# Attention and two MLPs on one core: a and b products of three batches moved ahead of the last transposes

## The chip, the cores and the metric

The kernel runs on one core of one Trainium2 chip. The metric is the device time of one execution in microseconds (us), lower is better. Names of the engines: PE is TensorE (PEld its weight loads), DVE is VectorE, ACT is ScalarE, POOL is GpSimd, SP is SyncE, which here only issues DMAs.

## The reference

Three blocks in a row, all in float32 with float64 MLP weights that the kernel splits itself:

```
a    = softmax over the sequence of phi              # 4 batches, 8 heads, 576 positions, 32 memories
k_m  = a^T k,  v_m = a^T v                           # 32 x 64 per head
attn = softmax(q k_m^T / 8) over the 32 memories
x    = attn v_m                                      # as 2304 tokens x 512
x    = ((x @ w_a) * (x @ w_b)) @ w_out               # 512 -> 1536 -> 512
x    = elu(x @ w_in) @ w_out2                        # 512 -> 2048 -> 512
```

## The kernel before

Precision is kept by splitting each float32 operand of a matmul in two float32r parts, hi and lo, and adding three products (hi hi, hi lo, lo hi). The kernel is one hand-written order: inside `tc.manual_schedule()` each engine executes its instructions in the order in which the Python code records them, and semaphores hold an instruction until its inputs are there and its output buffer is free.

**First stage, a loop over the four batches i.** `stage_kv` makes k_m and v_m from a and the loaded k, v (L360), `stage_turn`, `stage_kT` and `stage_vT` turn them, `stage_scores(i-1)` makes the scores of the batch before (L401, L405), `stage_aT(i+1)` transposes a of the next one (L336, evicted by ACT at L340), `stage_softmax` subtracts the maximum (DVE, L427, L429) and takes the exponential (ACT, L431), `stage_norm` divides by the sums (DVE, L445 to L451) and `stage_xT` transposes the result by PE (L462, L466) and splits it into `xhi` (ACT, L69) and `xlo` (DVE, L70). So softmax(b) is recorded in round b+1, norm(b) and xT(b) in round b+2; what is left of batches 2 and 3 stands behind the loop.

**u.** The product attn v_m w_a is done as attn (v_m w_a). `step_u(f, .., bs)` makes u = v_m w for a block f of 128 hidden units and some batches: two halves of 12 matmuls each on PE (L489), each rounded to hi by ACT (L504) and to lo by DVE (L500, one step later by `defer`) into the one buffer `ur`; behind the second `lower` the function `spread` issues four DMAs on SP for each batch (L513), which bring u into the partitions where the next matmul wants it. `step_u(0)` is done in two pieces, batches 0 and 1 in round 3, batches 2 and 3 behind the loop.

**ab.** `steps_ab(f, b)` has two parts of 12 matmuls each (L629): part 0 gives a, which ACT copies to `a_sb` (L636); part 1 gives b, by which DVE multiplies a (L638). One and two steps later ACT and DVE split the product into gh (L639) and gl (L640). 12 blocks f by 4 batches follow each other; `step_u(f+1)` stands behind batch 1 of block f, and `run_o1` (L671) takes up to three finished blocks of a batch into the output y of the first MLP. The second MLP follows (`step_h`, `steps_o2`).

**Weights.** Each weight block (a unit, 512 KB of float64) is loaded by POOL's DMA queue into one of two `raw` buffers (L103) and worked into hi and lo by seven pieces, which `fill(n)` records between other steps. Within unit n: slot 1 takes hi of unit n-1 (ACT, L133), slot 2 its lo (DVE, L142), slot 3 frees the raw buffer and issues the load of unit n+2, slot 4 has ACT convert the low words of unit n+1 (L119), slot 5 its magnitude (L113); the other slots are DVE alone (L155, L158, L163, L168, L173, L176). In the first stage `FILLS` gives the number of pieces for each round, and in the ab steps it is `RATE_AB`, one piece for each part.

**PSUM.** Up to the end of the first stage there are two tiles of two banks (`ps0`, taken by `pstile`) and four of one bank (`ps1`, by `pone`); then `ps1` is closed, and `ps2` gives two more of two banks.

**The end of the first stage** (L581 to L613): u of batches 2 and 3, scores of batch 3, norm and xT of batch 2, softmax and norm of batch 3 in buffers that are borrowed from the pool `pb` (hence the list in `both`, and an identity made again by POOL in `small`); then in the loop over f and b ab(0,0), ab(0,1), u of block 1, xT of batch 3, ab(0,2), ab(0,3), ab(1,0).

Of the kernel before, what the change touches and what calls it, by code (L numbers as in the profile page):

```python
# [21 lines left out]
def attention_then_two_mlps(ctx, tc, q, kv, kv_left, phi, w_ab, w_o1, w_i2, w_o2, out):  # L22
# [179 lines left out]
    FILLS = 6, 6, 6, 6  # L202
# [220 lines left out]
    def stage_softmax(b):  # L423

        for (ps, n, ng), (at, mx, _) in zip(st.pop(("sc", b)), st["at", b]):
            mx = mx[0:n]
            nc.vector.tensor_reduce(out=mx, in_=ps, op=ALU.max, axis=AX.X)  # L427
            for o, i, m in both(at, n, ps, mx):
                nc.vector.tensor_tensor(out=o, in0=i, in1=m.to_broadcast(list(o.shape)), op=ALU.subtract)  # L429
            for o, in both(at, n):  # L430
                nc.scalar.activation(out=o, in_=o, func=AF.Exp, scale=SCALE)  # L431

    def both(at, n, *others):

        if isinstance(at, list):
            yield from ([at[u][0:n], *[x[:, u] for x in others]] for u in range(2))
        else:
            yield [at[0:n], *others]

    def stage_norm(b, eng):  # L440

        parts = [(at, sm[0:n], n) for (at, _, sm), n in zip(st["at", b], (P, LEFT))]
        for at, sm, n in parts:
            for o, m in both(at, n, sm):
                nc.vector.tensor_reduce(out=m, in_=o, op=ALU.add, axis=AX.X)  # L445
        for at, sm, n in parts:
# [25 lines left out]
    def step_u(f, amount, bs=tuple(range(B))):  # L472
# [7 lines left out]
        def half(k):  # L480
# [15 lines left out]
            src = ps.rearrange("p i (c n) -> p i c n", c=2)  # L496
            hi, lo = [ur[:, :, 2 * k:2 * k + 2, x] for x in range(2)]
# [18 lines left out]
        half(0)  # L516
        half(1)

    with tc.manual_schedule():
# [79 lines left out]
        small = pb.tile([P, S], F32R, tag="gl", name="small", bufs=9).bitcast(F32)  # L599
        ats = [pb.tile([P, S], F32R, tag="gh", name=f"at{u}", bufs=9).bitcast(F32) for u in range(2)]  # L600
        ats = [t[:, 0:4 * NJ * M].rearrange("p (g m) -> p g m", m=M) for t in ats]
        als = [small[:, u * P:(u + 1) * P].rearrange("p (g m) -> p g m", m=M) for u in range(2)]
        st["ident"] = small[:, 2 * P:3 * P]
# [292 lines left out]
```

## Time and profile before

| | us |
|---|---|
| three executions, median (lowest, highest) | 838.73 (837.79, 839.49) |
| the profiled execution, its own time | 838.2 |
| its span, first to last instruction | 836.4 |
| PE busy in it | 794.7 |
| DVE busy in it | 610.3 |

The rows read for the prediction stand in a section of their own below. A line of the timeline gives start, duration, engine, line of the kernel, operation, output<-input, shapes and count, and in brackets how long the engine had been idle and what released it. All times count from the start of the span.

### The profile page before, as it was taken

The numbers are of one execution on the slowest core, as the hardware profiler recorded it, in microseconds if no ns is written. First come the engines' busy times: TensorE is split into PE (matmuls) and PEld (weight loads), VectorE is DVE, ScalarE is ACT, GpSimd is POOL, SyncE is SP. The second block draws the span as 40 slices with busy tenths as digits, with TensorE's granted clock in tenths as the row PEclk, the third lists the DMA queues.
The fourth block names the chain that finished last, engine by engine and source line by source line (L and its number), as shares of the span: only waits on it lengthen the run. The fifth ranks groups of instructions, "written<-read, shape, count | busy, mean of one in ns | idle before, by whom it ended". The sixth has DMA issues, their size and how long they took to land.

```text
span 836.4 us, 13805 instructions
## 1 busy us (share of the span) xinstructions
PE 794.7 (95%) x5576; PEld 739.7 (88%) x5576; DVE 610.3 (73%) x1015; ACT 413.6 (49%) x636; POOL 43.1 (5%) x91
## 2 busy tenths in 40 slices
PE   4686799999999999999999999999999999999998
PEld 3575789999999999999999898889998889998896
DVE  4497877878887888567788852887777876776555
ACT  4354456655454444334358753566554565543360
POOL 3000000000000000000000000000000000000000
PEclk9598899999999999999999999999999999999999
DMA  9973267664775277516001200111111110100006
GB/s 302 367 252 91 61 161 178 159 152 109 176 175 125 80 177 177 125 30 150 26 1 51 74 27 1 53 49 52 50 51 51 51 51 25 51 26 1 1 1 226
DMA packets 32175, 82.95 MB, mean 99 GB/s; under 512 B 4848, under 2 KB 4848, under 8 KB 32112
## 3 DMA queue, kind: packets, MB, share of 16 engines
q1 hardware_dynamic: 22320, 46.41, 20.5%
q0 software_dynamic: 9792, 35.66, 14.4%
q8 instruction: 44, 0.72, 0.4%
q14 instruction: 19, 0.16, 0.1%
HBM read 52.17 MB, written 4.72 MB: 68 GB/s over the span
## 4 chain that ended last, share of the span: by engine, by line
PE 87%; DVE 4%; DMA 4%; ACT 2%; issue 1%; SPq 1%; POOL 1%; DVEq 0%; ACTq 0%; POOLq 0%
PE o_ps L796 24%; PE h_ps L753 24%; PE o_ps L671 17%; PE ab_ps L629 16%; DMA raw<-in_w_ab_dram 3%; PE u_ps L489 2%; PE sc L401 2%; PE pk L360 1%; DVE ur L500 1%; SPq L513 1%; DMA u<-ur 1%; DVE a_sb L638 0%; DVE at L429 0%; ACT gh L639 0%; DVE a L163 0%
## 5 line engine op out<-in xcount | busy, mean ns | idle before, releaser
L629 PE MATMUL ab_ps<-xhi,u 128*128 128x288 f32 x768 | 141.0, 301 | 5.3 <-DVE ur L500 2.6
L629 PEld LDWEIGHTS ab_ps<-xhi,u 128*128 128x128 f32 x768 | 116.1, 192 | 7.4 <-DVE ur L500 3.0
L796 PE MATMUL o_ps<-ulh,g2h 128*128 128x512 f32 x288 | 114.2, 397 | 0.0
L796 PE MATMUL o_ps<-ull,g2h 128*128 128x512 f32 x288 | 114.2, 396 | 0.0
L796 PE MATMUL o_ps<-ulh,g2l 128*128 128x512 f32 x288 | 103.5, 397 | 0.0
L771 DVE SCALAR_TENSOR_TENSOR e<-e,th 128x768 f32<-128x768 f32 x48 | 46.0, 959 | 76.5 <-ACT e L768 76.2
L753 PE MATMUL h_ps<-yh,usl 128*128 128x384 f32 x384 | 98.2, 336 | 0.0
L753 PE MATMUL h_ps<-yh,ush 128*128 128x384 f32 x384 | 98.1, 336 | 0.0
L753 PE MATMUL h_ps<-yl,ush 128*128 128x384 f32 x384 | 98.1, 336 | 0.0
L764 ACT ACTIVATE e<-h_ps 128x768 f32<-128x768 f32 x48 | 39.0, 812 | 96.1 <-PE h_ps L753 94.1
L629 PE MATMUL ab_ps<-xlo,u 128*128 128x288 f32 x384 | 83.3, 299 | 0.0
L671 PE MATMUL o_ps<-gh,ulh 128*128 128x288 f32 x384 | 83.0, 297 | 0.1
L671 PE MATMUL o_ps<-gh,ull 128*128 128x288 f32 x384 | 82.4, 296 | 0.0
L671 PE MATMUL o_ps<-gl,ulh 128*128 128x288 f32 x384 | 82.4, 295 | 0.0
L753 PEld LDWEIGHTS h_ps<-yh,ush 128*128 128x128 f32 x384 | 69.7, 188 | 1.3
L753 PEld LDWEIGHTS h_ps<-yh,usl 128*128 128x128 f32 x384 | 69.5, 188 | 0.0
L753 PEld LDWEIGHTS h_ps<-yl,ush 128*128 128x128 f32 x384 | 69.5, 188 | 0.0
L638 DVE TENSOR_TENSOR a_sb<-a_sb,ab_ps 128x576 f32<-128x576 f32 x48 | 36.1, 753 | 42.2 <-PE ab_ps L629 35.7
L796 PEld LDWEIGHTS o_ps<-ulh,g2l 128*128 128x128 f32 x288 | 54.2, 188 | 13.2
L796 PEld LDWEIGHTS o_ps<-ull,g2h 128*128 128x128 f32 x288 | 54.3, 188 | 12.5
L796 PEld LDWEIGHTS o_ps<-ulh,g2h 128*128 128x128 f32 x288 | 54.3, 188 | 12.5
L629 PEld LDWEIGHTS ab_ps<-xlo,u 128*128 128x128 f32 x384 | 63.0, 192 | 0.0
(115 smaller groups left out, 1385.2 us busy)
## 6 DMA issues: line engine op xcount, KB each, us to landing
u<-ur SPq DMA_DIRECT2D x192, 128.0 KB, 5.0
raw<-in_w_o_dram POOLq DMA_DIRECT2D x28, 512.0 KB, 4.1
raw<-in_w_ab_dram POOLq DMA_DIRECT2D x24, 512.0 KB, 5.6
kv_t<-in_kv_dram SPq DMA_DIRECT2D x16, 512.0 KB, 8.4
raw<-in_w_i_dram POOLq DMA_DIRECT2D x16, 512.0 KB, 3.7
q_t<-in_q_dram SPq DMA_DIRECT2D x8, 576.0 KB, 9.9
out_dram<-y SPq DMA_DIRECT2D x8, 512.0 KB, 2.9
phi_t<-in_phi_dram SPq DMA_DIRECT2D x3, 576.0 KB, 10.4
```

The source lines that it names most:

```text
L360: nc.tensor.matmul(pk[M * h:M * h + M, D * u:D * u + D], a[0:P if j < NJ else LEFT, u, j, M * h:M * h + M], rows, start=(j == 0), stop=(j ...
L401: nc.tensor.matmul(sc[:, u, j * P:(j + 1) * P], qs[u][:, t, j * P:(j + 1) * P], kt[:, u, t * P:(t + 1) * P], start=(t == 0), stop=(t == 1))
L489: nc.tensor.matmul(ps[:, i, c * 256:c * 256 + 256], v[r, 2 * k + c].rearrange("p b m -> p (b m)"), w[r, c * 256:c * 256 + 256], start=(n = ...
L500: nc.vector.tensor_tensor(out=lo, in0=src, in1=hi.bitcast(F32), op=ALU.subtract)
L513: nc.sync.dma_start(out=us[b][o:o + M].rearrange("p k h n -> p k (h n)").bitcast(F32), in_=src.bitcast(F32))
L629: nc.tensor.matmul(ps[:, h, 0:HS], u[:, kk, w, n * P:n * P + P], x[b][:, kk, h * HS:(h + 1) * HS], start=(kk == 0 and i == 0), stop=(kk == ...
L638: nc.vector.tensor_tensor(out=a_sb, in0=a_sb, in1=ps[:, :, 0:HS], op=ALU.mult)
L671: nc.tensor.matmul(ps[:, h, 0:HS], w[:, cc], g[:, h * HS:(h + 1) * HS], start=(n == 0 and i == 0), stop=(n == len(fs) - 1 and i == 2),)
L753: nc.tensor.matmul(ps[:, h, 0:HB], w[:, c], x[:, c, h * HB:(h + 1) * HB], start=(c == 0 and i == 0), stop=(c == KC - 1 and i == 2),)
L764: nc.scalar.activation(out=e, in_=ps[:, :, 0:HB], func=AF.Relu, scale=-1.0)
L771: nc.vector.scalar_tensor_tensor(out=e, in0=e, scalar=1.0, in1=th, op0=ALU.add, op1=ALU.mult)
L796: nc.tensor.matmul(ps[:, k, :], g[:, c * P:(c + 1) * P], w, start=(f == fs[0] and i == 0), stop=(f == fs[-1] and i == 2),)
```

## The change

- Behind the loop the order is now: scores of batch 3, part 0 of ab(0,0), norm and xT of batch 2, softmax of batch 3, the `xlo` of batch 2, part 1 of ab(0,0), u of batches 2 and 3, ab(0,1), norm of batch 3, ab(0,2), xT of batch 3. Then u of block 1 and ab(0,3). These first six ab parts carry no pieces of the weights.
- For that, a_sb and three of the nine gh and gl buffers come from a new pool `pg` that is opened where the pool of k, v and phi ends (round 3); q gets its own pool. xT of batches 2 and 3 uses three one-bank PSUM tiles.
- Softmax and norm of batch 3 use the ordinary tiles: one instruction where two halves stood, and no second identity.
- `FILLS` goes from 6, 6, 6, 6 to 8, 10, 6, 6, and in round 0 the pieces are recorded last, behind `stage_aT(1)`, `a_max(2)` and `a_exp(2)`.
- u is rounded only in the partitions of its own batches (64 of 128 in the two pieces of block 0).

```diff
-    FILLS = 6, 6, 6, 6
+    FILLS = 8, 10, 6, 6
...
-    def stage_xT(b):
+    def stage_xT(b, single=False):
+
         (at, _, _), (al, _, _) = st.pop(("at", b))
-        tp, tl = pstile("tp_x"), pone("tl_x")
...
+        if single:
+            tps, tl = [pone("tp_x") for _ in range(2)], pone("tl_x")
+        else:
+            tp, tl = pstile("tp_x"), pone("tl_x")
+            tps = [tp[:, u] for u in range(2)]
...
+        for c, u, src in parts:
+            nc.scalar.activation(out=xhi[b][:, u, c], in_=src, func=AF.Copy)
+
+        def lower():
+            for c, u, src in parts:
+                nc.vector.tensor_tensor(out=xlo[b][:, u, c], in0=src, in1=xhi[b][:, u, c].bitcast(F32), op=ALU.subtract)
+
+        return lower
...
-            src = ps.rearrange("p i (c n) -> p i c n", c=2)
-            hi, lo = [ur[:, :, 2 * k:2 * k + 2, x] for x in range(2)]
+            r = slice(M * bs[0], M * bs[-1] + M)
+            src = ps[r].rearrange("p i (c n) -> p i c n", c=2)
+            hi, lo = [ur[r, :, 2 * k:2 * k + 2, x] for x in range(2)]
...
+        def parts_ab(f, b, amount):
...
+            pool, nb = (pg, NG) if turns_g[0] % 9 < NG else (pb, 9 - NG)
...
+            return [lambda: part(0), lambda: part(1)]
...
+            if i == B - 1:
+                es_l.close()
+                pg = es_g.enter_context(tc.tile_pool(name="pg", bufs=3, reuse_waits="tile"))
...
-            fill(FILLS[i])
+            if i:
+                fill(FILLS[i])
...
+            if i == 0:
+                fill(FILLS[0])
+
+        last = B - 1
+        stage_scores(last)
+        ab = parts_ab(0, 0, 0)
+        ab[0]()
+        stage_norm(last - 1, nc.vector)
+        lower_x = stage_xT(last - 1, True)
+        soft_tiles(last)
+        stage_softmax(last)
+        lower_x()
+        ab[1]()
         step_u(0, 0, (2, 3))
-        tick()
-        stage_scores(B - 1)
-        stage_norm(B - 2, nc.vector)
-        stage_xT(B - 2)
-
-
-        last = B - 1
-        es_l.close()
+        steps_ab(0, 1, 0)
+        stage_norm(last, nc.vector)
+        steps_ab(0, 2, 0)
+        stage_xT(last, True)()
+        es_q.close()
...
             for b in range(B):
-                if (f, b) == (0, 2):
-                    flush_later()
-                    stage_xT(last)
-                steps_ab(f, b, RATE_AB)
+                if f or b > 2:
+                    steps_ab(f, b, RATE_AB)
                 if f + 1 < NF1 and b == 1:
                     step_u(f + 1, 2 * RATE_U)
```

What this moves in the order of the engines, at three places.

**ACT in rounds 0 and 1.** Before, behind `vthi` of batch 0 (`ush` is a weight's hi, `lw` the low words of unit 2, `a_t` the eviction of the transposes of a for batch 1, `m` of k_m and v_m):

```order
L391 ACTIVATE vthi<-pt 128x4x32
L133 ACTIVATE ush<-a 128x512
L119 ACTIVATE lw<-raw 128x512
L340 ACTIVATE a_t<-tp_a 128x2x512
L343 ACTIVATE a_t<-tl_a 64x2x128
L314 ACTIVATE phi_t,sm<-phi_t,nm 128x576 x2
L367 ACTIVATE m<-pk 128x128 x2
```

Now, the same place, and round 1 up to the eviction for batch 2 (the lines count three more):

```order
L394 ACTIVATE vthi<-pt 128x4x32
L343 ACTIVATE a_t<-tp_a 128x2x512
L346 ACTIVATE a_t<-tl_a 64x2x128
L317 ACTIVATE phi_t,sm<-phi_t,nm 128x576 x2
L134 ACTIVATE ush<-a 128x512
L120 ACTIVATE lw<-raw 128x512
L114 ACTIVATE a<-raw 128x512
L370 ACTIVATE m<-pk 128x128 x2
L389 ACTIVATE kt_99<-pt 128x2x64 x2
L394 ACTIVATE vthi<-pt 128x4x32
L134 ACTIVATE ush<-a 128x512
L120 ACTIVATE lw<-raw 128x512
```

The eviction `a_t` for batch 1 stands ahead of `lw` of unit 2. The last row is `lw` of unit 3, which stood in round 2 before; behind it come L114, L134 and the eviction for batch 2.

**DVE behind the loop.** Before, from the end of softmax(2) (`smx`, `sl`) to xT(2) (`xlo_82`); `ur` is the lo of u of batches 2 and 3:

```order
L429 TENSOR_TENSOR at<-sl,smx 64x256
L500 TENSOR_TENSOR ur<-u_ps,ur 128x2x2x256 x2
L445 TENSOR_REDUCE ssm<-at 128x32
L445 TENSOR_REDUCE ssm<-at 64x8
L447 TENSOR_SCALAR ssm<-ssm 128x32
L448 RECIPROCAL ssm<-ssm 128x32
L447 TENSOR_SCALAR ssm<-ssm 64x8
L448 RECIPROCAL ssm<-ssm 64x8
L451 TENSOR_TENSOR at<-at,ssm 128x1024
L451 TENSOR_TENSOR at<-at,ssm 64x256
L70 TENSOR_TENSOR xlo_82<-tp_x,xhi_78 128x2x512
```

Now, from the end of norm(2): softmax(3), `xlo` of batch 2 (here `xlo_85`), the product of ab(0,0), its gl, the two lo of u, the product of ab(0,1), norm(3):

```order
L443 TENSOR_TENSOR at<-at,ssm 64x256
L430 TENSOR_REDUCE smx<-sc 128x32
L431 TENSOR_TENSOR at<-sc,smx 128x1024
L430 TENSOR_REDUCE smx<-sl 64x8
L431 TENSOR_TENSOR at<-sl,smx 64x256
L465 TENSOR_TENSOR xlo_85<-tp_x,xhi_81 128x512 x2
L465 TENSOR_TENSOR xlo_85<-tl_x,xhi_81 128x2x64
L565 TENSOR_TENSOR a_sb<-a_sb,ab_ps 128x576
L567 TENSOR_TENSOR gl<-a_sb,gh 128x576
L500 TENSOR_TENSOR ur<-u_ps,ur 64x2x2x256 x2
L565 TENSOR_TENSOR a_sb<-a_sb,ab_ps 128x576
L438 TENSOR_REDUCE ssm<-at 128x32
```

The two `ur` stood ahead of norm(2); now they stand behind softmax(3).

**PE around u of block 1.** Before, from the last matmuls of that u (the `small` rows are xT of batch 3; `xhi_78` is batch 2):

```order
L489 MATMUL u_ps<-ush,vtlo 128x256 x2
L462 MATMUL tp_x<-small,at_1060 128x128 x4
L462 MATMUL tp_x<-small,at_1061 128x128 x4
L466 MATMUL tl_x<-small 128x64 x2
L629 MATMUL ab_ps<-xhi_78,u 128x288 x2
L629 MATMUL ab_ps<-xlo_82,u 128x288 x2
```

Now, from the end of ab(0,2) (here `xhi_81`):

```order
L556 MATMUL ab_ps<-xlo_85,u 128x288 x2
L556 MATMUL ab_ps<-xhi_81,u 128x288 x2
L455 MATMUL tp_x<-ident,at 128x128 x8
L457 MATMUL tl_x<-ident,at 128x64 x2
L488 MATMUL u_ps<-ush,vthi 128x256 x2
L488 MATMUL u_ps<-usl,vthi 128x256 x2
```

u of block 1 had ab(0,2) and ab(0,3), four parts, between itself and its first reader ab(1,0); now it has ab(0,3) alone, two parts.

## Rows read from the trace of the kernel before

**Rows 1.** The page: the span.
```profile
span 836.4 us, 13805 instructions
```

**Rows 2.** Timeline of PE, 49 to 125 us.
```profile
49.39 1.06 PE L462 MATMUL tp_x<-ident,at 128*128 128x128 f32 x8 [1.42 <-DVE at L451]
...
65.20 1.09 PE L462 MATMUL tp_x<-ident,at 128*128 128x128 f32 x8 [1.66 <-DVE ur L500]
...
67.31 3.84 PE L401 MATMUL sc<-kt,q_t 128*128 128x128 f32 x32
...
79.79 5.44 PE L401 MATMUL sc<-kt,q_t 128*128 128x128 f32 x32 [4.13 <-DVE ur L500]
...
89.85 0.72 PE L629 MATMUL ab_ps<-xhi,u 128*128 128x288 f32 x2 [2.30 <-DVE xlo L70]
...
103.72 0.85 PE L629 MATMUL ab_ps<-xhi,u 128*128 128x288 f32 x2 [2.61 <-DVE ur L500]
...
124.34 0.39 PE L489 MATMUL u_ps<-ush,vthi 64*128 64x256 f32 x2 [1.21 <-ACT y L679]
```

**Rows 3.** Windows: stretch, length, busy of PE, PEld, DVE, ACT, POOL; PEclk, DMA share, GB/s.
```profile
36.00:38.00 2.00, 2.00 (x13) 1.67 (x10) 0.74 (x3) 1.17 (x4) 0.00 (x0) 0.50 1.05 416
65.20:72.10 6.90, 6.89 (x66) 6.20 (x67) 5.66 (x11) 3.47 (x8) 1.18 (x3) 1.00 0.45 92
79.80:83.20 3.40, 3.40 (x16) 3.40 (x17) 3.33 (x8) 0.00 (x0) 0.00 (x0) 0.50 0.28 66
89.90:93.40 3.50, 3.50 (x15) 3.50 (x16) 3.43 (x7) 1.71 (x5) 0.00 (x0) 0.52 0.00 0
```

**Rows 4.** Timeline of ACT, 24 to 80 us.
```profile
24.50 0.65 ACT L119 ACTIVATE lw<-raw 128x512 bf16<-128x512 uint32 x1 [2.29 <-DMA raw<-in_w_ab_dram]
25.06 1.00 ACT L340 ACTIVATE a_t<-tp_a 128x1024 f32<-128x1024 f32 x1
...
77.46 1.94 ACT L504 ACTIVATE ur<-u_ps 128x1024 fp32r<-128x1024 f32 x2 [1.52 <-DMA u<-ur]
```

**Rows 5.** Timeline of DVE, 26 to 112 us.
```profile
26.56 1.41 DVE L308 TENSOR_REDUCE nm<-phi_t 128x1 f32<-128x576 f32 x2 [2.55 <-DMA phi_t<-in_phi_dram]
...
41.41 1.22 DVE L427 TENSOR_REDUCE smx<-sc 128x32 f32<-128x1024 f32 x1 [0.83 <-PE sc L401]
...
59.71 1.54 DVE L445 TENSOR_REDUCE ssm<-at 128x32 f32<-128x1024 f32 x2 [0.46 <-ACT at L431]
...
61.90 1.50 DVE L451 TENSOR_TENSOR at<-at,ssm 128x1024 f32<-128x1024 f32 x2
...
72.06 1.22 DVE L427 TENSOR_REDUCE smx<-sc 128x32 f32<-128x1024 f32 x1
...
74.89 0.42 DVE L429 TENSOR_TENSOR at<-sl,smx 64x256 f32<-64x256 f32 x1
...
102.45 2.35 DVE L500 TENSOR_TENSOR ur<-u_ps,ur 128x1024 fp32r<-128x1024 f32 x2
...
111.96 0.75 DVE L638 TENSOR_TENSOR a_sb<-a_sb,ab_ps 128x576 f32<-128x576 f32 x1 [1.38 <-PE ab_ps L629]
```

**Rows 6.** Tile raw, 23 to 25 us: the load of unit 3 (durations in ns).
```profile
L163 DVE SCALAR_TENSOR_TENSOR a<-raw,a x1: 684/684/684, 22.9 to 22.9; 128x512 uint32<-128x512 uint32 x1
L103 POOL DMA_DIRECT2D raw<-in_w_ab_dram x1: 527/527/527, 24.1 to 24.1; - x1
...
DMA to landing us min/median/max: 9.9/9.9/9.9
```

**Rows 7.** Tile raw, 0 to 130 us: its ten loads.
```profile
DMA to landing us min/median/max: 3.7/7.2/10.3
```

**Rows 8.** Tile ur on SP, 80 to 104 us: the DMAs of u, batches 2, 3.
```profile
L513 SPq DMA_DIRECT2D u<-ur x8: 585/596/602, 80.9 to 85.4; - x8
...
DMA to landing us min/median/max: 2.3/2.3/4.0
```

**Rows 9.** Tile ur on SP, 71.9 to 72.6 us: the last two for batches 0, 1.
```profile
DMA to landing us min/median/max: 5.3/5.4/5.5
```

**Rows 10.** Chain that ended last, 60 to 180 us: start, us, what.
```profile
61.91 0.93 PE u_ps L489 x12
...
161.25 9.58 PE ab_ps L629 x72
```

More of the change, by code (lines that the diff above doesn't have):

```diff
@@ L247, in attention_then_two_mlps @@
     p0 = es_0.enter_context(tc.tile_pool(name="p0", bufs=2, side="right", reuse_waits="tile"))
+    es_q = ExitStack()
+    pq = es_q.enter_context(tc.tile_pool(name="pq", bufs=2, side="right", reuse_waits="tile"))
     es_l = ExitStack()
@@ L425, in stage_softmax @@
         for (ps, n, ng), (at, mx, _) in zip(st.pop(("sc", b)), st["at", b]):
-            mx = mx[0:n]
+            at, mx = at[0:n], mx[0:n]
             nc.vector.tensor_reduce(out=mx, in_=ps, op=ALU.max, axis=AX.X)
[L428 to L438, printed above, removed]
@@ L440, in stage_norm @@
-    def stage_norm(b, eng):
[L442 to L446, printed above, removed]
+            nc.vector.tensor_tensor(out=at, in0=ps, in1=mx.to_broadcast(list(at.shape)), op=ALU.subtract)
+            nc.scalar.activation(out=at, in_=at, func=AF.Exp, scale=SCALE)
+    def stage_norm(b, eng):
+        parts = [(at[0:n], sm[0:n]) for (at, _, sm), n in zip(st["at", b], (P, LEFT))]
+        for at, sm in parts:
+            nc.vector.tensor_reduce(out=sm, in_=at, op=ALU.add, axis=AX.X)
+        for at, sm in parts:
@@ L447, in stage_norm @@
             nc.vector.tensor_scalar(out=sm, in0=sm, scalar1=1e-9, scalar2=None, op0=ALU.add)
             nc.vector.reciprocal(out=sm, in_=sm)
-        for at, sm, n in parts:
-            for o, m in both(at, n, sm):
-                eng.tensor_tensor(out=o, in0=o, in1=m.to_broadcast(list(o.shape)), op=ALU.mult)
-    def stage_xT(b):
+        for at, sm in parts:
+            eng.tensor_tensor(out=at, in0=at, in1=sm.to_broadcast(list(at.shape)), op=ALU.mult)
+    def stage_xT(b, single=False):
@@ new lines, in stage_xT @@
+        parts = [(slice(0, SM), u, tps[u]) for u in range(2)] if single else [(slice(0, SM), slice(0, 2), tp)]
+        parts.append((slice(SM, S), slice(0, 2), tl[:, 0:2 * LEFT].rearrange("p (u s) -> p u s", u=2)))
+        for c, u, src in parts:
[3 more added lines that the diff above has]
+                nc.vector.tensor_tensor(out=xlo[b][:, u, c], in0=src, in1=xhi[b][:, u, c].bitcast(F32), op=ALU.subtract)
@@ L514, in spread, with step_u @@
                                           in_=src.bitcast(F32))
-        half(0)
-        half(1)
+        return [lambda: half(0), lambda: half(1)]
+    def step_u(f, amount, bs=tuple(range(B))):
+        for half in halves_u(f, amount, bs):
+            half()
     with tc.manual_schedule():
@@ L532, in attention_then_two_mlps, with part, pe, evac @@
                     nc.gpsimd.tensor_copy(out=pair[:, odd, i, M * c:M * c + M], in_=heads[:, c ^ odd, i])
-        st["ident"] = ident
+        es_g = ExitStack()
+        turns_g = [0]
+        def parts_ab(f, b, amount):
+            u = u_t.pop((f, b))
+            a_sb = pg.tile([P, 2, HS], F32, tag="a_sb", name="a_sb", bufs=3)
+            flat = a_sb.rearrange("p a s -> p (a s)")
+            pool, nb = (pg, NG) if turns_g[0] % 9 < NG else (pb, 9 - NG)
+            turns_g[0] += 1
+            gh = pool.tile([P, S], F32R, tag="gh", name="gh", bufs=nb)
+            gl = pool.tile([P, S], F32R, tag="gl", name="gl", bufs=nb)
+            g_t[f, b] = gh, gl
+            def part(n):
+                ps = pstile("ab_ps")
+                def pe():
+                    for kk in range(2):
+                        for i, (w, x) in enumerate(((0, xhi), (0, xlo), (1, xhi))):
+                            for h in range(2):
+                                nc.tensor.matmul(
+                                    ps[:, h, 0:HS], u[:, kk, w, n * P:n * P + P], x[b][:, kk, h * HS:(h + 1) * HS],
+                                    start=(kk == 0 and i == 0), stop=(kk == 1 and i == 2),
+                                )
+                def evac():
+                    if n == 0:
+                        nc.scalar.activation(out=a_sb, in_=ps[:, :, 0:HS], func=AF.Copy)
+                    else:
+                        nc.vector.tensor_tensor(out=a_sb, in0=a_sb, in1=ps[:, :, 0:HS], op=ALU.mult)
+                        defer(1, lambda: nc.scalar.activation(out=gh, in_=flat, func=AF.Copy))
+                        defer(2, lambda: nc.vector.tensor_tensor(
+                            out=gl, in0=flat, in1=gh.bitcast(F32), op=ALU.subtract))
+                step(pe, evac, amount)
+            return [lambda: part(0), lambda: part(1)]
+        def steps_ab(f, b, amount):
+            for part in parts_ab(f, b, amount):
+                part()
         more_loads()
@@ L597, in attention_then_two_mlps @@
         pb = es_b.enter_context(tc.tile_pool(name="pb", bufs=2, side="right", reuse_waits="tile"))
[L599 to L603, printed above, removed]
```

52 lines of the change are left out of this document (7 added, 45 removed).

## The prediction

> **What bounds the kernel now.** I read the page first: the span is 836.4 us [rows 1], PE is busy in 794.7 us of it. So PE is the bound, and what can be won is its idle time and the time in which it runs below its clock. The timeline of PE shows where both are: between 49 and 125 us there are gaps of 1.42, 1.66, 4.13, 2.30, 2.61 and 1.21 us [rows 2]. The windows give the granted clock behind them: 1.00 behind the gap of 1.66, but 0.50 behind 4.13 and 0.52 behind 2.30 [rows 3], the lower of the two levels (1.2 of 2.4 GHz). What that costs is in one pair of rows: the same 32 matmuls of the scores take 3.84 us at full clock and 5.44 behind the gap of 4.13 [rows 2], 1.6 us more.
>
> Then ACT and DVE, for what ends these gaps. The gap of 4.13 is ended by a DVE lo of u (L500), which waits for the hi on ACT (L504), which stood still for 1.52 us until the DMAs of the u before had left the single buffer `ur` [rows 4]: two of those took 5.3 to 5.5 us [rows 9], where an undisturbed one takes 2.3 [rows 8]. The gap of 2.61 at ab(0,2) is again an L500. In the first rounds the DMA is full: 416 GB/s, a share of 1.05, at 36 to 38 us [rows 3].
>
> The profiled execution took 838.2 us, 0.5 below the median of 838.73. I sum against 838.2 and add the 0.5. About 0.2% (1.7 us) is what a measurement of this kernel can tell from no change.
>
> **Part A, the pieces in rounds 0 and 1.** Before, ACT waits for the raw data of unit 2 until 24.50 (2.29 us idle), and the eviction `a_t` of batch 1 stands behind that `lw`, at 25.06 [rows 4]. Now the eviction is first, and can run in those idle 2.29 us, some 3 us earlier. I cost this at nothing: k_m and v_m of batch 1 then wait for their loads under the full DMA, and the scores of batch 0 for them. What is late next is unit 3. DVE's pieces of round 0 now stand behind `a_max(2)`, which waits for phi until 26.56 and ends at 27.97 [rows 5]; four pieces and the one that frees the buffer, at most 0.68 each [rows 6], put the issue of unit 3's raw load at about 31.3 instead of 24.1 [rows 6]. POOL issues nothing else there. And its `lw` is needed earlier: round 1 has ten pieces instead of six, and they stand ahead of softmax(0) on DVE.
>
> Loads of raw took 3.7 to 10.3 us, 7.2 in the median [rows 7]; this very load took 9.9 [rows 6], with the DMA as full as it will be at 31 to 38. I take 8.5, between the median and that row: it lands at 39.8. Then `lw` (0.65 [rows 4]) and five pieces, some of them beside each other on ACT and DVE and none over 0.68, together 2.5: softmax(0) starts at 43.0 instead of 41.41 [rows 5], **+1.5**. With 7.2 it is +0.2, with 9.9 it is +2.9. If the load came so early that only DVE's own work counts, the ten pieces would end at 39.5, and softmax(0) would be 1.9 early; this is the lower end. DVE carries the shift on: norm(0) ends the gap before xT(0) [rows 2], scores(1) follow.
>
> A second cost: ACT stands at `lw` and has the eviction for batch 2 behind it, and PE has no other work before xT(0). The gap there is 1.42 [rows 2]; I get about 2.4, between 1.66 (clock kept) and 2.61 (the ab behind it slowed: its first two matmuls 0.85 for 0.72). Half clock over the following block costs up to 1.6 by the pair of scores; I take half, **+0.8** (0 to 1.6). Part A: +2.3.
>
> By the Trainium skill, page "DMA: Bandwidth & Descriptors", section "Queues, rings and completion order", each DMA engine takes turns, packet by packet, between the queues that have work, so that a load on POOL's queue would get a share of its own beside SP's queue. By that the load would land far sooner, and Part A would be a gain; this is the first rival below. The 9.9 us of the load under a full DMA speaks against it.
>
> **Part B, behind the loop.** I place the new order by durations from the rows, on the time base of before: scores 3.84 [rows 2], 12 matmuls of u 0.93, an ab part of 12 matmuls 9.58/6 = 1.60 [rows 10]; softmax on DVE 72.06 to 75.31 (3.25), norm 59.71 to 63.40 (3.69) [rows 5]; two hi of u on ACT 1.94 [rows 4], two lo 2.35, a product 0.75 [rows 5]; an issue on SP 0.60, landing 2.3 [rows 8].
>
> PE has scores(3) right behind scores(2), which end at about 72.1: to 76.9 with their tail, part 0 of ab(0,0) to 78.5. The 4.13 gap is gone. DVE: softmax(2) to 75.3, norm(2) to 79.3. PE waits 0.6 for it, does xT(2) to 80.45, part 1 to 82.05 and the first half of u(2,3) to 83.0. DVE's softmax(3) then runs to 82.6, `xlo` to 84.0, the product to 84.65, which frees the PSUM of the second half of u: PE waits 1.75. The two lo of u end at 87.2 and 88.4; ab(0,1) starts after another 1.55 of waiting and ends at 90.45. The DMAs of u (four issues, 2.3 to land) let ab(0,2) start at 92.75, after a gap of 2.3, to 95.95. xT(3) to 97.3, u of block 1 to 99.5, its lo to 103.65 (before: 102.45 + 2.35 = 104.80 [rows 5]), ab(0,3) to 102.7.
>
> Here the new order has its weak place: only ab(0,3) lies between u of block 1 and its reader. u lands in its place at 103.65 + 0.1 + three more issues (1.93 with the steps between) + 2.3 = 108.0, so PE waits 5.3 us before ab(1,0), where it did not wait before. Even so ab(1,0) starts at 108.0. Before, it followed ab(0,3) without a gap, and the end of that is marked by its product, which waited for PE until 111.96 [rows 5]; I take 111.7 for its start, a little before that product: **-3.7**.
>
> Three prices come on top. The piece that frees the buffer for unit 7 now stands between the two lo, so its raw load is issued at about 103.1, just ahead of the DMAs of u: these could take 5.4, as the pair in [rows 9], instead of 2.3. A load of that size alone costs the DMA some 1.3 us (512 KB at 416 GB/s [rows 3]); I take **+1.2** (0 to 3.1). Half clock behind the gap of 5.3, longer than the 4.13 that lost it: **+1.6** (0 to 1.6). Half clock at ab(0,2) behind 2.3, the length of the gap that lost it at ab(0,0): its end is on the path to u of block 1 only in part, **+0.4** (0 to 1.6). Part B: -3.7 + 3.2 = -0.5, between -3.7 and +2.6.
>
> **Part C, the rest.** Rounds 0 and 1 hold six pieces more, the first six ab parts none; from ab(0,3) on the count is the same. In the gap before ab(1,0) DVE works ahead, and the wait of 1.21 for y at the next u [rows 2] may shrink: **-0.6** (-1.2 to 0).
>
> **At nothing:** the second identity (POOL has only issues of DMAs besides); softmax(3) in one instruction for two halves (0.2 us of DVE, inside its 3.25); u rounded on 64 partitions, 1.2 each for 1024 elements in 128 partitions (down to -1.2 if the two take half; I take no gain, since an eighth of the elements, 64x256 at L429, took 0.42, a third of the 1.22 of 128x1024 [rows 5], so the number of partitions counts for little); the pools, which have as many buffers as before.
>
> **Sum:** +2.3 - 0.5 - 0.6 = +1.2, so 839.4 by the profiled execution, **839.9** by the median.
>
> **Rivals.**
> - *The raw load gets its share* (faster). With half of the DMA it lands after about 5.0 us (3.7, the shortest of [rows 7], and 1.3), at 36.3; DVE's pieces then end at 39.5. Part A is -1.9 and its gap does not grow: -1.9 - 0.5 - 0.6 = -3.0, **835.7**. For it: the shortest load; against: 9.9 and 1.05 of share.
> - *An undisturbed end of the stage* (faster). The DMAs of u take 2.3 and the clock comes back at once: B is -3.7, the sum 2.3 - 3.7 - 0.6 = -2.0, **836.7**. For it: eight DMAs of u with 2.3 in the median [rows 8], and the clock at 1.00 behind 1.66; against: half clock behind every gap of 2.3 and more.
> - *Half clock at each new gap* (slower). PE meets gaps at xT(0), ab(0,2) and ab(1,0); if each ends at the lower clock, A is 1.5 + 1.6 = 3.1, B is -3.7 + 1.2 + 1.6 + 1.6 = +0.7, and C gains nothing: +3.8, **842.5**. It decides from gaps of about 2 us on (1.66 kept the clock, 2.30 did not). For it: [rows 3]; against: the gap at xT(0) may stay below that.
>
> That the change does not do what it says can be left out: the orders of the engines show it.
>
> **How the numbers follow.** Forecast 839.9: 0.35; its own range is 838.3 to 840.4, within 0.2% of before. The raw load early 0.17, the undisturbed end 0.15: faster 0.32. Half clock at each gap 0.33: slower. As both signs hold most of the chance, the range takes in the rivals: low end the early load with the other half of C, 835.7 - 0.6 = 835.1; high end the half clock with the load at 9.9, 842.5 + 1.4 = 843.9. The sums of all lower and all upper ends, about -6 and +7, are left out.
>
> **What would show it.** Right: the `a_t` eviction of batch 1 ends before 23 us; ACT waits at `lw` for the raw data of unit 3 until about 40; softmax(0) starts at 43; no gap before scores(3); ab(1,0) starts at about 109 behind a gap of 5 or more that ends with the DMA of u, at a clock of 0.5. Wrong: softmax(0) before 41.4 (first rival); a gap under 3 before ab(1,0), or the clock at 1.00 behind it (second); gaps behind the loop that I do not have, of ACT above all, would make it worse than all cases.

## The result and the profile after

| | before | after |
|---|---|---|
| median of four executions of each on the same chip, us | 838.51 | 843.24 |
| lowest and highest | 837.79, 839.49 | 842.01, 843.74 |
| ratio, 95% interval | | 1.006 (1.004 to 1.0079) |
| the profiled execution, its own time | 838.2 | 842.0 |
| its span | 836.4 | 840.2 |

The change makes the kernel 4.7 us slower. The forecast was 839.9, "within 0.2%"; the time lies inside the range (835.1 to 843.9), and close to the rival "half clock at each new gap", 842.5. The profiled execution is the fastest of its four, so the trace has 3.8 of the 4.7 us to show. The order of PE says where they lie. Its timeline after (the columns are those of [rows 2]):

```profile
31.36 0.37 PE L363 MATMUL pk<-kv_t,a_t 128*32 128x64 f32 x2 [2.13 <-issue]
...
33.55 5.48 PE L404 MATMUL sc<-kt,q_t 128*128 128x128 f32 x32
...
50.57 1.86 PE L455 MATMUL tp_x<-ident,at 128*128 128x128 f32 x8 [4.54 <-DVE at L443]
...
54.20 3.84 PE L404 MATMUL sc<-kt,q_t 128*128 128x128 f32 x32
...
67.91 1.09 PE L455 MATMUL tp_x<-ident,at 128*128 128x128 f32 x8 [1.64 <-DVE ur L500]
...
70.02 3.84 PE L404 MATMUL sc<-kt,q_t 128*128 128x128 f32 x32
...
74.80 3.84 PE L404 MATMUL sc<-kt,q_t 128*128 128x128 f32 x32
...
81.82 1.09 PE L455 MATMUL tp_x<-ident,at 128*128 128x128 f32 x8 [0.36 <-DVE at L443]
...
87.37 0.39 PE L488 MATMUL u_ps<-ush,vthi 64*128 64x256 f32 x2 [1.51 <-DVE a_sb L565]
...
90.14 0.53 PE L556 MATMUL ab_ps<-xhi,u 128*128 128x288 f32 x2 [1.80 <-DVE ur L500]
...
95.63 0.51 PE L556 MATMUL ab_ps<-xhi,u 128*128 128x288 f32 x2 [0.56 <-DMA u<-ur]
...
113.83 0.82 PE L556 MATMUL ab_ps<-xhi,u 128*128 128x288 f32 x2 [7.38 <-DMA u<-ur]
...
119.38 0.43 PE L685 MATMUL o_ps<-gh,ulh 128*128 128x288 f32 x2
...
126.64 0.39 PE L488 MATMUL u_ps<-ush,vthi 64*128 64x256 f32 x2 [0.73 <-ACT y L693]
...
128.78 0.39 PE L488 MATMUL u_ps<-ush,vthi 64*128 64x256 f32 x2 [1.15 <-ACT y L693]
...
137.68 0.42 PE L685 MATMUL o_ps<-gh,ulh 128*128 128x288 f32 x2
```

The same places in the kernel before, for the difference:

```profile
36.41 4.97 PE L401 MATMUL sc<-kt,q_t 128*128 128x128 f32 x32
...
51.47 3.84 PE L401 MATMUL sc<-kt,q_t 128*128 128x128 f32 x32
...
114.89 0.43 PE L671 MATMUL o_ps<-gh,ulh 128*128 128x288 f32 x2
...
132.28 0.42 PE L671 MATMUL o_ps<-gh,ulh 128*128 128x288 f32 x2
...
146.25 0.39 PE L489 MATMUL u_ps<-ush,vthi 64*128 64x256 f32 x2 [0.63 <-ACT a_sb L636]
```

Read the two as a running account. In round 1 scores(0) come 2.86 us earlier (33.55 for 36.41), and yet xT(0) starts 1.18 us later (50.57 for the 49.39 of [rows 2]); scores(1) 2.73 later, since xT(0) and what follows it ran slowly: 3.63 us from the one to the other, where before they took 2.08. Scores(2) are still 2.71 late (70.02 for 67.31). Then the new order does what it should: scores(3) follow at once, the gap of 4.13 is gone, and the next gaps are 0.36, 1.51, 1.80 and 0.56. But ahead of ab(1,0) PE waits 7.38 us, and ab(1,0) itself takes 5.55 (113.83 to 119.38) where 24 such matmuls take 3.2. At the first matmul of the output (L685) the change is 4.49 late, at the second half of u of block 2 4.44 (128.78 for 124.34). That half stands behind two waits for y, of 0.73 and 1.15 us, and behind them PE runs at half clock for 3.2 us, where the kernel before kept its clock (1.00 from 125.4 to 128.4): at the next output the change is 5.40 late (137.68 for 132.28). Of these 5.4 us 1.6 come back, about half of them because two gaps of the kernel before, 0.15 at 139 us and 0.63 at 146, no longer appear.

The windows give the clock at xT(0), at ab(0,1), at ab(1,0) and behind u of block 2 (columns as in [rows 3]):

```profile
50.60:54.20 3.60, 3.60 (x27) 2.87 (x27) 2.33 (x8) 1.19 (x2) 0.00 (x0) 0.53 0.70 279
91.60:95.00 3.40, 3.40 (x15) 3.12 (x14) 0.00 (x0) 0.65 (x1) 0.00 (x0) 0.51 0.66 152
113.80:119.00 5.20, 5.17 (x22) 5.20 (x23) 0.00 (x0) 1.74 (x3) 0.00 (x0) 0.51 0.86 203
129.30:132.50 3.20, 3.20 (x18) 2.98 (x17) 2.61 (x5) 3.20 (x5) 0.00 (x0) 0.50 0.41 150
```

PE is busy throughout all four and has half its clock, 1.2 of 2.4 GHz. At ab(0,1) this costs nothing, since the next matmuls wait for u in any case (0.56 at 95.63). What PE waited for stands on the other engines: ACT in round 1, POOL's two raw loads, DVE between the two lo of u of block 1, and the first four DMAs of that u.

```profile
39.92 0.68 ACT L120 ACTIVATE lw<-raw 128x512 bf16<-128x512 uint32 x1 [5.07 <-DMA raw<-in_w_ab_dram]
```
```profile
31.80 0.53 POOL L104 DMA_DIRECT2D raw<-in_w_ab_dram  x1 [15.11 <-DVE p L169]
...
106.26 0.53 POOL L104 DMA_DIRECT2D raw<-in_w_o_dram  x1 [32.27 <-ACT lw L120]
```
```profile
42.59 1.22 DVE L430 TENSOR_REDUCE smx<-sc 128x32 f32<-128x1024 f32 x1
...
103.90 1.22 DVE L500 TENSOR_TENSOR ur<-u_ps,ur 128x1024 fp32r<-128x1024 f32 x1
105.03 0.68 DVE L164 SCALAR_TENSOR_TENSOR a<-raw,a 128x512 uint32<-128x512 uint32 x1
105.64 1.22 DVE L500 TENSOR_TENSOR ur<-u_ps,ur 128x1024 fp32r<-128x1024 f32 x1
```
```profile
L513 SPq DMA_DIRECT2D u<-ur x4: 585/598/604, 106.9 to 108.8; - x4
...
DMA to landing us min/median/max: 4.9/5.0/5.2
```

The raw load of unit 7 is issued at 106.26, 0.6 us ahead of the first DMA of u, which then land in 4.9 to 5.2 us.

### The profile page after: what moved, and what is told of

The parts are those of the page before. It is cut to its first block, busy times and chain, and to the rows that moved or that the text cites. A ratio compares the mean times of both kernels' runs of the same rounds, so it can differ in the third digit from the quotient of the medians.

```text
span 840.2 us, 13789 instructions
## 1 busy us (share of the span) xinstructions
PE 797.9 (95%) x5576; PEld 742.5 (88%) x5576; DVE 610.3 (73%) x1011; ACT 414.4 (49%) x636; POOL 42.4 (5%) x89
## 4 chain that ended last, share of the span: by engine, by line
PE 88%; DVE 5%; DMA 4%; ACT 2%; issue 1%; SPq 0%; DVEq 0%; ACTq 0%
PE o_ps L809 24%; PE h_ps L766 24%; PE o_ps L685 18%; PE ab_ps L556 18%; PE u_ps L488 2%; DMA phi_t<-in_phi_dram 2%; DMA raw<-in_w_ab_dram 1%; PE pk L363 1%; DMA u<-ur 1%; DVE ur L500 1%; DVE ssm L438 1%; DVE at L431 1%; DVE smx L430 0%; PE tp_x L455 0%; PE sc L404 0%
## 5 line engine op out<-in xcount | busy, mean ns | idle before, releaser
L556 PE MATMUL ab_ps<-xhi,u 128*128 128x288 f32 x768 | 142.7, 303 | 9.7 <-DMA u<-ur 7.9
L685 PE MATMUL o_ps<-gh,ulh 128*128 128x288 f32 x384 | 82.5, 296 | 0.2
L685 PE MATMUL o_ps<-gh,ull 128*128 128x288 f32 x384 | 82.4, 296 | 0.0
L685 PE MATMUL o_ps<-gl,ulh 128*128 128x288 f32 x384 | 82.3, 296 | 0.0
L565 DVE TENSOR_TENSOR a_sb<-a_sb,ab_ps 128x576 f32<-128x576 f32 x48 | 36.1, 753 | 53.5 <-PE ab_ps L556 49.4
L563 ACT ACTIVATE a_sb<-ab_ps 128x576 f32<-128x576 f32 x48 | 31.3, 651 | 75.2 <-PE ab_ps L556 75.1
```

The lines of the kernel that those rows point to most:

```text
L556: nc.tensor.matmul(ps[:, h, 0:HS], u[:, kk, w, n * P:n * P + P], x[b][:, kk, h * HS:(h + 1) * HS], start=(kk == 0 and i == 0), stop=(kk == ...
L563: nc.scalar.activation(out=a_sb, in_=ps[:, :, 0:HS], func=AF.Copy)
L565: nc.vector.tensor_tensor(out=a_sb, in0=a_sb, in1=ps[:, :, 0:HS], op=ALU.mult)
L685: nc.tensor.matmul(ps[:, h, 0:HS], w[:, cc], g[:, h * HS:(h + 1) * HS], start=(n == 0 and i == 0), stop=(n == len(fs) - 1 and i == 2),)
```

## The experiments

Executions of one kernel spread over several microseconds (the kernel before went from 834.6 to 840.2 in 31), so times below are medians, each against the kernel before in the same chip session; behind it stand the ratio and its 95% interval. The change itself is +4.7 (1.004 to 1.0079). Where a mechanism is at stake I read the run's own trace, by stretches within it.

**The pieces put back.** The change with the pieces where they were:

```diff
-    FILLS = 8, 10, 6, 6
+    FILLS = 6, 6, 6, 6
...
-            if i:
-                fill(FILLS[i])
+            fill(FILLS[i])
...
-        ab = parts_ab(0, 0, 0)
+        ab = parts_ab(0, 0, RATE_AB)
...
```

> The changed kernel with the weight pieces recorded as before: 6 in each round, round 0's in the old place, and one for each of the first six ab parts. Theory (the moved pieces cost 2.7 us: softmax(0) 1.2 us late behind the raw load of unit 3, then a gap of 4.5 at xT(0) and half clock, 1.5): xT(0) starts at about 49.4 at full clock, scores(3) at about 72.1, and the time is 843.2 - 2.7 = 840.5, plus up to 1 for the pieces that DVE now has between the products: 840.5 to 841.5. Rival (the delay comes from the order behind the loop alone, or the pieces cost as much there as they do in round 1): within 0.8 us of 843.2.

841.13 against 838.23, +2.9 (ratio 1.0037, 1.0019 to 1.0056). In its trace the gap at xT(0) is 1.42 again, as before the change, but xT(0) starts at 50.22 and not at 49.4, the clock behind it was low all the same, and the pieces lengthen the stretch behind the loop:

```profile
50.22 1.75 PE L455 MATMUL tp_x<-ident,at 128*128 128x128 f32 x8 [1.42 <-DVE at L443]
...
87.59 0.39 PE L488 MATMUL u_ps<-ush,vthi 64*128 64x256 f32 x2 [2.12 <-DVE a_sb L565]
...
115.69 0.82 PE L556 MATMUL ab_ps<-xhi,u 128*128 128x288 f32 x2 [6.03 <-DMA u<-ur]
```

By the medians 1.8 of the 4.7 us go with the moved pieces, but the two intervals overlap, and the profiled execution (842.58, above the median of its run) does not show the gain: ab(1,0) starts at 115.69, where the change has 113.83. What is clear is that the order behind the loop with its old pieces is still slower than the kernel before. Undoing the pieces is no cure, since they then stand in DVE's way between the products (2.12 for 1.51).

**The moved pieces alone, in the kernel before.**

```diff
-    FILLS = 6, 6, 6, 6
+    FILLS = 8, 10, 6, 6
...
-                steps_ab(f, b, RATE_AB)
+                steps_ab(f, b, RATE_AB if f or b > 2 else 0)
```

(and round 0's pieces recorded last, as in the change).

> The kernel before with this one part of the change: 8, 10, 6, 6 pieces, round 0's recorded last, none in the first six ab parts. Theory: round 1 is late by the same 2.7 us (xT(0) behind a gap of about 4.5, at half clock), and the six pieces that leave the end of the stage give back 0 to 1: 838.5 + 2.7 - 0.5 = 840.7 (840 to 841.2). Rival (pieces ahead are a gain, the loss lies behind the loop): 838.5 or less.

839.77, +1.5 (1.0023, 1.0008 to 1.0037): slower, though by 0.7 less than the 2.2 expected. Round 1 cost more than expected and the end of the stage gave back more: xT(0) came behind a gap of 3.13 and took 1.94 us for 1.06, and scores(2) were 3.83 late (71.14 for 67.31); behind the loop the gap ahead of scores(3) was 3.31 for 4.13, that ahead of ab(0,2) 1.67 for 2.61, and the output was 2.42 late (117.31 for 114.89). The rival, that pieces ahead are a plain gain, falls. This +1.5 and the +2.9 of the run before add up to 4.4 of the 4.7: each part of the change loses by itself.

**The raw load of unit 3 early.** The change, with five of the eight pieces ahead of `a_max(2)`, where DVE waits for phi anyway:

```diff
+            if i == 0:
+                fill(5)
             if i + 2 < B:
                 a_max(i + 2, 0)
...
-                fill(FILLS[0])
+                fill(FILLS[0] - 5)
```

> The changed kernel with the first five of round 0's eight pieces recorded ahead of a_max(2), where DVE waits 5.2 us for phi, so that the raw load of unit 3 is issued at about 26.3 instead of 31.8. Theory (softmax(0) is late because that load is): ACT's wait at lw of unit 3 goes from 5.1 us to under 1, softmax(0) starts by 41, xT(0)'s gap is 3 us or less: 1.2 to 2.7 us faster than the change, 840.5 to 842. Rival (the load takes its bytes from those of k and v of batch 1, which now land later by as much): scores(0) starts 1 to 2 us later, the sum is zero, 843.

838.37 against 838.11, +0.3 (1.0009, 0.9993 to 1.0026): 4.4 us better than the change, by this one edit. Its POOL, ACT, DVE and PE:

```profile
25.59 0.53 POOL L104 DMA_DIRECT2D raw<-in_w_ab_dram  x1 [8.76 <-DVE a L164]
```
```profile
35.58 0.67 ACT L120 ACTIVATE lw<-raw 128x512 bf16<-128x512 uint32 x1 [2.64 <-DMA raw<-in_w_ab_dram]
```
```profile
38.25 1.22 DVE L430 TENSOR_REDUCE smx<-sc 128x32 f32<-128x1024 f32 x1
```
```profile
46.23 1.88 PE L455 MATMUL tp_x<-ident,at 128*128 128x128 f32 x8 [2.11 <-DVE at L443]
...
109.45 0.82 PE L556 MATMUL ab_ps<-xhi,u 128*128 128x288 f32 x2 [7.30 <-DMA u<-ur]
```

The load is issued 6.2 us earlier and there 4.3 earlier; softmax(0) starts 4.3 earlier, xT(0) too, and the 4.3 us reach ab(1,0) whole (109.45 for 113.83), with its gap unchanged. It is more than the 1.2 to 2.7 I expected, although ACT still waits 2.64 us at `lw`, where I had under 1: softmax(0), which in the kernel before waits for scores(0) until 41.41 [rows 5], can now use that these come earlier (31.63 for 36.41), and xT(0) is 3.2 us earlier even than in the kernel before. That the early load delays k and v (the rival) is not seen: the last matmuls on k of batch 1, at 31.36 in the change, stand at 29.44 in this run. The place of softmax(0) does not hang on one trace: it starts between 38.18 and 40.11 in the four runs with this load early, and between 41.76 and 42.72 in the six that have the change's first rounds as they are.

**The raw load of unit 7 early.** Three pieces moved from u of block 1 and ab(0,3) to ab(0,1), where DVE waits for PE:

```diff
-        steps_ab(0, 1, 0)
+        ab = parts_ab(0, 1, 0)
+        ab[0]()
+        fill(3)
+        ab[1]()
...
-                    steps_ab(f, b, RATE_AB)
+                    steps_ab(f, b, RATE_AB if f else 0.5)
...
-                    step_u(f + 1, 2 * RATE_U)
+                    step_u(f + 1, 2 * RATE_U if f else 0)
```

> The changed kernel with three pieces, among them the one that issues the raw load of unit 7, moved from u of block 1 and ab(0,3) to ab(0,1), where DVE waits 3.9 us. Theory (u of block 1 lands late because that raw load stands ahead of its DMAs, 4.9 us instead of 2.3, and because its piece stands between the two lo, 0.6): ab(1,0) starts 2.5 to 3.2 us earlier, its gap is about 4.5 and still ends at half clock: 843.2 - 2.8 = 840.4. Rival (the sixteen DMAs of u in a row are their own crowd): landing stays near 4.9, only the 0.6 is won: 842.6.

839.4 against 838.23, +1.2 (1.0019, 1.0002 to 1.0035), 3.5 us better than the change. The load went out at 94.7; the two lo of u ran in one piece, and of its DMAs the first four were:

```profile
L513 SPq DMA_DIRECT2D u<-ur x4: 585/596/600, 105.4 to 107.4; - x4
...
DMA to landing us min/median/max: 2.3/2.3/2.3
```
```profile
109.84 0.82 PE L556 MATMUL ab_ps<-xhi,u 128*128 128x288 f32 x2 [4.08 <-DMA u<-ur]
```

2.3 us to land instead of 5, and a gap of 4.08 instead of 7.38; the 3.3 between them are 2.6 of landing and some 0.7 of the two lo, which end that much earlier. So the DMAs of u were late because of the raw load ahead of them, and not because of their own number.

**The gap ahead of ab(1,0) filled.** Part 1 of ab(0,3) runs its matmuls five times, only the last pass counts:

```diff
-                    for kk in range(2):
+                    again = 5 if (f, b, n) == (0, 3, 1) else 1
+                    for kk in [0, 1] * again:
```

> The changed kernel with the 12 matmuls of part 1 of ab(0,3) run five times into the same PSUM tile (each pass starts it anew), so that PE works through 6.4 of the 7.4 us before ab(1,0). Theory (ab(1,0) takes 5.55 instead of 3.2 us because the clock fell in the gap): ab(1,0) starts at the same 113.8 at a clock of 1.00 and takes 3.2: 843.2 - 2.35 = 840.9, less if the late product of ab(0,3) costs DVE something (up to 0.7). Rival (its matmuls are slow because the data of u come one DMA after another): ab(1,0) still takes over 5 us, 843 or more.

840.66 against 838.23, +2.4 (1.004, 1.0024 to 1.0056), by the medians 2.3 better than the change although PE does more. ab(1,0) starts no earlier, but at full clock:

```profile
113.58 0.51 PE L557 MATMUL ab_ps<-xhi,u 128*128 128x288 f32 x2 [0.61 <-DMA u<-ur]
...
116.84 0.43 PE L686 MATMUL o_ps<-gh,ulh 128*128 128x288 f32 x2
```
```profile
113.60:116.80 3.20, 3.20 (x24) 3.20 (x25) 1.26 (x3) 1.35 (x3) 0.00 (x0) 1.00 0.88 207
```

3.26 us instead of 5.55: the half clock behind that gap costs 2.3 us. The 24 matmuls run without a wait from the same start, so the rival, data of u that come one DMA after another, falls.

**The gap ahead of xT(0) filled** in the same way, with the last of the four groups of matmuls on k and v of batch 2 run five times.

```diff
-        for j in range(NJ + 1):
+        again = 5 if (b, n, u) == (2, 0, 1) else 1
+        for j in list(range(NJ + 1)) * again:
```

> The changed kernel with the last of the four groups of k_m and v_m of batch 2 run five times into the same PSUM tile, so that PE works through 3.9 of the 4.5 us ahead of xT(0). Theory (half clock behind that gap costs 1.55 us): xT(0) to scores(1) take 2.1 instead of 3.6 us, 843.2 - 1.5 = 841.7. Rival (the clock is no matter of this gap, as behind gaps of 1.4 to 1.5 in other runs it was low as well): no change, 843.2.

849.66 against 838.44, +11.2: a miss. The repeated group did not fit the gap; it ran mostly at the lower clock itself, so xT(0) started at 55.32 and found the clock low as well:

```profile
42.00:55.30 13.30, 10.54 (x320) 7.75 (x312) 9.28 (x20) 3.17 (x8) 0.00 (x0) 0.63 0.83 290
55.40:59.00 3.60, 3.60 (x26) 2.91 (x26) 0.62 (x1) 1.47 (x3) 0.00 (x0) 0.51 0.02 5
```

What the clock at xT(0) hangs on stays open, and the 1.55 us that I put on it have no run of their own. Behind gaps of 1.42 to 1.48 us it was full (before), half (the pieces put back) or in between (the two fastest kernels below): there the gap alone does not decide.

**u of block 1 first.** The change with the three pieces early, and u of block 1 ahead of the transposes of batch 3:

```diff
         steps_ab(0, 2, 0)
+        step_u(1, 0)
+        tick()
         stage_xT(last, True)()
```

> The changed kernel with u of block 1 ahead of the transposes of batch 3 instead of behind them, both its lo at once, and the three pieces moved as in the run with unit 7's load early. Theory (ab(1,0) waits for u of block 1, which begins too late): u of block 1 begins about 1.4 us earlier on PE and its lo no longer wait for the xlo of batch 3, so ab(1,0) starts about 2.6 us earlier than with the early load alone, and with a gap under 1 us, so at full clock, 2.3 more: 839.4 - 4.9 = 834.5, or 835.3 if a new gap ahead of ab(0,3), which now waits for batch 3's transposes, costs some clock. Rival (the wait only moves to ab(0,3) and its transposes, with its half clock): 838 or more.

837.58 against 838.11, -0.5 (0.9993, 0.9977 to 1.0008): 5.3 us better than the change, and by the medians 1.7 better than with the raw load early alone (the two intervals overlap). The gap ahead of ab(1,0) is gone. I expected 2 to 3 us more; they went to four waits that add up to 1.75 us at ab(0,3), for xhi and xlo of batch 3, and to half clock behind them (0.50 from 106.6 to 110.0), as the rival said:

```profile
104.59 0.37 PE L556 MATMUL ab_ps<-xhi,u 128*128 128x288 f32 x1 [0.44 <-ACT xhi L461]
105.13 0.40 PE L556 MATMUL ab_ps<-xhi,u 128*128 128x288 f32 x1 [0.17 <-ACT xhi L461]
...
106.27 0.40 PE L556 MATMUL ab_ps<-xlo,u 128*128 128x288 f32 x1 [0.74 <-DVE xlo L465]
107.07 0.61 PE L556 MATMUL ab_ps<-xlo,u 128*128 128x288 f32 x1 [0.40 <-DVE xlo L465]
```

**Four pieces in round 1**, on top of that: `FILLS = 8, 4, 6, 6`, and seven pieces in ab(0,1).

> As the run with u of block 1 first, and 4 pieces instead of 10 in round 1, so that nothing there needs the raw data of unit 3; seven pieces stand in ab(0,1), one in each part of ab(0,3). Theory: softmax(0) starts right behind scores(0), at about 39.2 instead of 42.6, xT(0) has a gap of about 1.5: 2.7 us under the run with u of block 1 first, 832. Rival (PE's clock or the later pieces take it back, as with the pieces back in place): no better than that run.

837.07, -1.0 (0.9987, 0.9974 to 1.0): softmax(0) started at 37.16 and waited for PE, xT(0) had a gap of 1.48; but seven pieces did not fit into ab(0,1), and a wait of 4.13 us for u came up at ab(0,2). The gain was given back there, as the rival said: the output begins at 114.16, for 114.55 in the run before.

**Both raw loads early**: u of block 1 first, the load of unit 3 ahead of `a_max(2)`, `FILLS = 8, 8, 6, 6`, five pieces in ab(0,1).

> As the run with u of block 1 first, with the load of unit 3 early as in the run for that, 8 pieces in round 1 and five in ab(0,1). Theory: 2 to 2.7 us under the run with u of block 1 first, 832 to 833. Rival (the early load delays k and v): no better than that run.

831.7 against 838.11, -6.4 (0.9924, 0.9903 to 0.9944): faster than both kernels, well clear of the noise.

```profile
46.98 1.32 PE L455 MATMUL tp_x<-ident,at 128*128 128x128 f32 x8 [1.48 <-DVE at L443]
...
110.14 0.43 PE L692 MATMUL o_ps<-gh,ulh 128*128 128x288 f32 x2
```

The output begins at 110.14, 4.75 us ahead of the kernel before.

**Its first rounds alone, on the old order.** The kernel before with round 0's pieces and the load of unit 3 as in the fastest run, 8, 8, 6, 6 pieces, and two in place of six in the first six ab parts.

> The kernel before, its order behind the loop kept, with the first rounds of the fastest run so far: a_t of batch 1 first, the load of unit 3 issued ahead of a_max(2), 8, 8, 6, 6 pieces. It tells what the order behind the loop is worth. Theory (the early rounds and the order behind the loop add up): softmax(0) starts at about 39, xT(0) 2.5 to 3 us earlier than in the kernel before: 838.1 - 2.7 = 835.4, and the new order behind the loop with u of block 1 first is worth the other 3.7 us. Rival (the new order alone makes the gain possible, the old one waits for ur and PSUM all the same): 837.5 or more.

835.55 against 838.44, -2.9 (0.9962, 0.9948 to 0.9977): by the medians the first rounds are worth 2.9 us by themselves. The other 3.5 are then the mended order behind the loop, by subtraction; that order was not run without them. Nor does the profiled execution (836.58, 1.0 above the median) show the 2.9 as a gain carried through: xT(0) starts at 46.17, 3.2 earlier than in the kernel before, but PE runs the 6.8 us behind it at half clock, and scores(3) start at 79.76 for the 79.79 of [rows 2]. The 1.6 us by which its span is shorter appear later; 1.3 of them between 122 and 146 us.

```profile
46.90:53.70 6.80, 6.71 (x41) 5.74 (x38) 5.59 (x13) 3.56 (x8) 0.53 (x1) 0.50 0.93 361
```

**gl behind the lo of u**, on the fastest kernel.

> The fastest run so far with gl of ab(0,0), which stands on DVE ahead of the two lo of u of batches 2 and 3, recorded behind them. Theory (those lo wait for it): ab(0,1)'s wait of 1.8 us shrinks by 0.8 to 1.5, and the u of batches 2 and 3 comes 0.6 us earlier: 831.7 - 0.6 = 831.1. Rival (they wait for ACT's hi anyway): no change, 831.7.

833.61 against 838.44, -4.8 (0.9933, 0.9914 to 0.9952): no gain. ab(0,1) waited 0.28 instead of 1.79, but then part 1 waited 0.74 for ACT and ab(0,2) 0.76 for u.

## Why the prediction was right or wrong

- **Part A, the place: right.** The chain came as told: the raw load of unit 3 issued at 31.80 (forecast 31.3), landed after 8.1 us (8.5), `lw` at 39.92 (39.8), softmax(0) at 42.59 (43.0). Only the eviction `a_t` came 2.1 us earlier (22.94 for 25.06) and not 3, so that it did not end before 23. By the rule of the Trainium skill (page "DMA: Bandwidth & Descriptors", section "Queues, rings and completion order") I had a rival in which this load gets half of the DMA and lands in 5 us. The traces do not bear that reading out: 8.1 us here (DMA share 1.02) and 10.0 with the load at 25.6 (1.03).
- **Part A, "the eviction is first ... I cost this at nothing": wrong.** With it scores(0) came forward, from 36.41 to 33.55 in the two traces, and they start between 31.63 and 34.43 in all eleven runs that have the eviction first, for 36.41 and 36.72 in the two that do not. With softmax(0) late this was no gain, but PE ran out of work earlier, and the gap at xT(0) became 4.54 us where I had 2.4. With the load in time, xT(0) came 3.2 us ahead of the kernel before; I take the earlier scores(0) for the reason, which was not tried apart. By the same step the -1.9 of my first rival could not be had in my own terms: softmax(0) waits for scores(0) until 41.41, and can start at 39.5 only if these come earlier. A step that arrives earlier is free only as long as its engine has work until the next wait.
- **Part A, half clock: under-sized.** I took half of 1.6 us; the stretch from xT(0) to scores(1) lost 1.55. Part A: +2.7 instead of +2.3. The rule "it decides from gaps of about 2 us on", which I had read from two rows, does not hold: in the trace after, PE kept its clock behind 1.64 (scores(2) behind it take 3.84), but not at ab(0,1) behind waits of 1.51 and 1.80, nor behind 0.73 and 1.15 at u of block 2. The length of the last gap alone does not decide.
- **Part B up to u of block 1: right.** With 2.7 added for Part A, my times for ab(0,0), xT(2), ab(0,1) and ab(0,2) (79.6, 81.8, 89.95, 95.45) were met within 0.2 us (79.59, 81.82, 90.14, 95.63). The half clock that I put at ab(0,2), 0.4, fell on ab(0,1) and was hidden by the wait for u.
- **Part B, the weak place: right in kind, too small in all three terms.** I had "PE waits 5.3", 1.2 for the raw load, 1.6 for the clock. The lo of u ended 0.5 later than forecast; the load cost the last DMA 2.6 (4.9 for 2.3) and not 1.2; the clock cost 2.3 and not 1.6, since it stayed low for the whole of ab(1,0). In place of -0.5, Part B was -0.6 at the start of ab(1,0) and, with 2.3 for its clock, +1.8 behind it.
- **Part C: the size right by luck (-0.7 for -0.6, from the output of 119.38 on):** the waits for y stayed (0.73 and 1.15 for 0.32 and 1.21). The half clock behind them, which I did not have, took the delay from 4.44 to 5.40 us at the next output; then 1.6 came back, most of it by 152 us of the kernel before.
- **The failed step** is the term of the landing of u, "I take +1.2 (0 to 3.1)", and after it the clock behind the same gap. The sum was 1.2 and the trace has 3.8; the 2.6 between them are 1.4 for the landing, 0.7 for that clock, 0.5 for the later lo and 0.4 for Part A, less 0.4 for ab(0,2). For the landing I had a row of the very case, the 5.4 us of [rows 9] (a raw load had gone out at 70.15 in that trace), and took the time of the load's bytes at 416 GB/s instead, which no row shows as the delay of another DMA. The slower rival had the mechanism, half clock behind the gaps; that its 3.8 is the measured 3.8 is partly luck, as it had 0.4 too much in Part A, 1.1 too little in Part B and missed the 0.7 of Part C. Three small slips change nothing: 43.0 for 41.41 is +1.6, the wait ahead of xT(2) is 0.8 by my own times (78.5 to 79.3), and all lower ends add up to -6.8.

## What to carry to other kernels

When pieces of a side job move, follow the transfer that one of them issues: here the loss was not the work of the pieces, but two loads, one issued 7.7 us later and needed a round earlier, the other issued just ahead of transfers that PE waits for. Both were mended by recording the issuing piece where DVE stood idle; with one reordered step and two pieces fewer in round 1 that turned +4.7 into -6.4 us. And price a wait of PE together with the clock behind it: the gap of 7.4 us cost 2.3 more in the stage that followed, and a gain of 3.2 us at xT(0) was lost again to half clock in the one trace of the first rounds alone.

## What the runs showed of the hardware

- The lo of u take 1.22 us each in 64 partitions as in 128 (the trace after, block 0 and block 1); rounding u in its own partitions saves nothing:

```profile
L500 DVE TENSOR_TENSOR ur<-u_ps,ur 64x1024 fp32r<-64x1024 f32 x4 | 4.7, 1218 | 0.6 <-ACT ur L504 0.5
...
L500 DVE TENSOR_TENSOR ur<-u_ps,ur 128x1024 fp32r<-128x1024 f32 x2 | 2.4, 1218 | 0.0
```

- One load of 512 KB, issued 0.6 us ahead, more than doubled the landing of the first four small DMAs behind it, on another queue: 4.9 to 5.2 us, for 2.3 in the run with that load early.
- A PE that works most of the time can have a low clock: 0.63 on average over 13.3 us of short matmuls, of which it was busy for 10.54, in the run with xT(0)'s gap filled. Filling a gap kept the clock where the filling was ab matmuls, and did not where it was matmuls on k and v (one run of each).
